# Bank reservation in the score filler, a GELU batch over chunks 3 and 4, and a new transpose estimate, in a two-layer attention and gMLP kernel

## The chip, the cores and the metric

The kernel runs on one core of one Trainium2 chip. The metric is the device time of one execution in microseconds (us), as the median of several runs. A ratio below is the mean time of one kernel's runs over the mean of the other's in the same rounds, so it is not quite the ratio of the medians quoted next to it. For every run the mean granted TensorE clock is recorded too (1.0 is full speed).

## The reference

Two layers, each an attention block and a gated mixer over x of 2048 x 512, bf16:

```python
def _A_ref(x, wq, wk, wv, wo):            # 32 heads of 16, one shared key and value head
    q = (x @ wq).reshape(B, S, 32, 16).transpose(0, 2, 1, 3)
    k = x @ wk;  v = x @ wv
    scores = einsum('bhqd,bkd->bhqk', q, k) * 16 ** -0.5
    o = einsum('bhqk,bkd->bhqd', softmax(scores), v)
    return o.transpose(0, 2, 1, 3).reshape(B, S, 512) @ wo
def _B_ref(x, w_in, w_sp, b_sp, w_out):
    z = gelu(x @ w_in)                    # 512 -> 1792
    z1 = z[..., :896]; z2 = layernorm(z[..., 896:])
    g = einsum('ts,bsf->btf', w_sp, z2) + b_sp[None, :, None]   # mixes tokens
    return (z1 * g) @ w_out
x = x + _A(layernorm(x)); x = x + _B(layernorm(x))      # twice, same weights
```

## The kernel before

The Python program holds a list scheduler. It models five engines in time (PE is TensorE, ACT ScalarE, DVE VectorE, POOL GpSimd, SP the DMA queue), and whenever a modelled engine is free it commits the ready operation of the lowest priority number. What it emits is a fixed order for each engine, with semaphore waits. So every number in the model can change the whole order.

A layer takes the queries in six chunks (512, 512, 512, 256, 128, 128 tokens). For each chunk come the scores, the exponentials, the products with V, the output projection, and then the first part of the mixer: two products with w_in, GELU, and the layernorm of z2. The product with w_sp runs in passes over the tiles of 128 tokens as they come ready: tiles 0 to 7 after chunk 1, 8 to 11 after chunk 2, 12 to 14 after chunk 4 (the "early pass"), tile 15 in the closing stage.

The exponentials, 4096 score blocks of 128 keys by 512 columns (tokens, or tokens times heads), are shared. Most go to ScalarE (an exp activate over 3 or 2 blocks). The others go to VectorE, which has a chain of seven instructions for them. A VectorE block rides along with a score fill: it takes one of the two side PSUM banks that all other products also use.

```python
class DexStream:
    def take(self, t, js):           # called when a score fill is committed: a VectorE block too?
        if sc.bank_free() > t:
            return None
        base = 2 * (self.nb % (NPD // 2))
        if not self.batch:
            ...
            backlog = sc.free["dve"] - t + sum(o.dur for o in sc.ready["dve"] ...)
            if backlog > BACKLOG:            # 3 us
                return None
        ...
    def limit(self, layer):          # no VectorE blocks in a layer's last units
        return len(self.k.units) * (layer + 1) // 2 - ENDX
```

GELU needs another ScalarE table set than exp, so it is done in batches. The products are copied out first; then one batch activates them in place. Chunks 0 and 1 share a batch; chunks 2, 3 and 4 have one each; chunk 5 activates straight from PSUM.

```python
def mixer_chunk(self, g):
    ...
    if g.ci == 0:
        self.held = (T, z1, z2, z1v)
        return
    zs = [(T[0], n, z1v)]
    if g.ci == 1:
        T, z1, z2 = [a + b for a, b in zip(self.held[:3], (T, z1, z2))]
        zs = [(T[0], n, self.held[3])] + zs
    ...
    def gl(e):
        for (_t, _n, v) in zs:
            e.activation(v, v, ACTF.Gelu_apprx_tanh)
        return e.activation(z2f[:, t0 * FH:(t0 + nt) * FH], z2f[...], ACTF.Gelu_apprx_tanh)
```

A DMA transpose is modelled as 1.25 us of issue, plus its bytes, plus 1.9 us until it is visible:

```python
def transpose(self, out, src, deps, sem, pr):
    return self.dma(lambda e: e.dma_start_transpose(out, src), deps, sem, 131072, pr, issue=1.25)
```

The softmax here doesn't subtract the row's maximum and nothing guards it: scores larger than these inputs give would overflow.

## Time and profile before

| | before |
|---|---|
| median time | 1871.99 us (3 runs, 1869.53 to 1872.58) |
| span of the profiled run | 1867.6 us |
| last exp of layer 0, of layer 1 | 880.5 us, 1812.6 us |
| score blocks on ScalarE, on VectorE | 3595, 501 |
| table loads | 21 |

These are lines of the page of before. The first gives busy us, share of the span and number of instructions of each engine. The others are groups of instructions: line, engine, operation, tiles and shapes, count, then busy us and mean ns of one, then the idle time just before them and what ended most of it.

```profile
PE 1595.0 (85%) x11889; PEld 477.3 (26%) x11889; DVE 1736.9 (93%) x3107; ACT 1756.6 (94%) x1581; POOL 53.4 (3%) x94
...
L1343 ACT ACTIVATE Pa<-ps_all 128x1536 bf16<-128x1536 f32 (+1 forms) x1439 | 1637.5, 1368 | 31.1 <-PE ps_all L1615 16.2
...
L1520 DVE TENSOR_SCALAR E<-ps_all 128x512 int32<-128x512 f32 x501 | 341.1, 683 | 28.8 <-PE ps_all L1615 26.3
```

Two engines are full. The 3595 blocks of ScalarE take 1637.5 us, 0.455 us each; the count of the last line is the number of blocks that VectorE takes.

The groups of ScalarE, kept apart by shape, show the table loads of the GELU batches (to GELU, and back to exp):

```profile
L993 ACT ACT_TABLE_LOAD x8 | 10.3, 1283 | 0.1
L1343 ACT ACT_TABLE_LOAD x8 | 10.3, 1283 | 0.1
```

The timeline of ScalarE around the batches of chunks 3 and 4 in layer 0. Its columns are start, time until the group's end, engine, line, operation; in brackets is the idle time before it and its releaser.

```profile
808.03 1.28 ACT L993 ACT_TABLE_LOAD   x1
809.32 1.70 ACT L993 ACTIVATE z1s<-z1s 128x1792 bf16<-128x1792 bf16 x1
810.93 1.68 ACT L994 ACTIVATE z2n<-z2n 128x1792 bf16<-128x1792 bf16 x1
812.62 1.28 ACT L1343 ACT_TABLE_LOAD   x1
813.92 19.29 ACT L1343 ACTIVATE Pa<-ps_all 128x1024 bf16<-128x1024 f32 x17
833.52 16.35 ACT L1343 ACTIVATE Pa<-ps_all 128x1536 bf16<-128x1536 f32 x14 [0.31 <-PE ps_all L1615]
...
852.44 1.28 ACT L993 ACT_TABLE_LOAD   x1
853.73 0.95 ACT L993 ACTIVATE z1s<-z1s 128x896 bf16<-128x896 bf16 x1
854.59 0.93 ACT L994 ACTIVATE z2n<-z2n 128x896 bf16<-128x896 bf16 x1
855.54 1.28 ACT L1343 ACT_TABLE_LOAD   x1
```

ScalarE runs through both batches without a pause.

Two stretches by engine (from:to in us, length, then busy us and instructions of each engine, granted TensorE clock, share and GB/s of DMA). The first lies in the steady part, the second holds chunk 4's batch.

```profile
core 0: us, PE busy (x) PEld busy (x) DVE busy (x) ACT busy (x) POOL busy (x), PEclk, DMA share, GB/s
93.00:117.00 24.00, 18.97 (x151) 4.76 (x144) 23.79 (x42) 23.94 (x22) 0.00 (x0) 1.00 0.00 1
846.00:857.00 11.00, 9.26 (x88) 3.79 (x86) 9.02 (x17) 10.76 (x11) 0.00 (x0) 1.00 0.05 12
```

### The profile page before, as it was taken

To read this page: it belongs to the slowest core of one execution; us is meant where nothing else is said; L and a number is where in the kernel's file an instruction comes from. 1 tells how busy PE (TensorE), PEld (TensorE's weight loads), DVE (VectorE), ACT (ScalarE), POOL (GpSimd) and SP (SyncE) were. 2 spreads that over 40 slices of the span, in tenths; PEclk is the share of its full clock that TensorE was granted. 3 is DMA by queue.
4 is the path that set the end of the run, shared out by engine and by line. 5 is a ranking of instruction groups with operands and counts; after the bars stand their busy time and mean duration, and the time that the engine had idled before them with its cause. 6 is when DMAs were issued, how large, how long until landed. Compare 5 with 4: busy or idle time off the path is not lost.

```text
span 1867.6 us, 30386 instructions
## 1 busy us (share of the span) xinstructions
PE 1595.0 (85%) x11889; PEld 477.3 (26%) x11889; DVE 1736.9 (93%) x3107; ACT 1756.6 (94%) x1581; POOL 53.4 (3%) x94
## 2 busy tenths in 40 slices
PE   8777888878889988989887778887788799999898
PEld 3222222212222222223432122222222222222234
DVE  8999999999879999997889999999999689989978
ACT  8999999999989999998579999999999899999983
POOL 2000000000000000000100000000000000000000
PEclk9999999999989999999999999999999899999999
DMA  9700010000010020221210000000000100111213
GB/s 272 197 1 1 12 35 1 1 1 18 7 40 24 23 46 1 66 70 48 66 33 1 1 1 12 10 26 1 5 13 7 40 24 24 46 43 35 62 45 110
DMA packets 125142, 68.58 MB, mean 37 GB/s; under 512 B 79172, under 2 KB 121416, under 8 KB 125000
## 3 DMA queue, kind: packets, MB, share of 16 engines
q1 hardware_dynamic: 123416, 66.48, 13.2%
q8 instruction: 95, 1.56, 0.3%
q14 instruction: 47, 0.39, 0.1%
q10 hardware_dynamic: 1584, 0.16, 0.1%
HBM read 30.97 MB, written 17.83 MB: 26 GB/s over the span
## 4 chain that ended last, share of the span: by engine, by line
ACT 36%; DVE 30%; PE 18%; issue 14%; POOL 1%; ACTq 0%; POOLq 0%; DVEq 0%
ACT Pa L1343 34%; PE ps_all L1088 6%; PE ps_all L1615 5%; DVE E L1520 5%; DVE Pd L1558 4%; PE ps_all L1419 3%; DVE E L1556 2%; DVE E L1553 2%; DVE E L1547 2%; DVE gp L1100 2%; PE ps_all L1177 1%; DVE st L622 1%; DVE E L1550 1%; DVE E L1549 1%; DVE z2n L937 1%
## 5 line engine op out<-in xcount | busy, mean ns | idle before, releaser
L1343 ACT ACTIVATE Pa<-ps_all 128x1536 bf16<-128x1536 f32 (+1 forms) x1439 | 1637.5, 1368 | 31.1 <-PE ps_all L1615 16.2
L1615 PE MATMUL ps_all<-qs,kT 32*128 32x512 bf16 x4096 | 566.5, 387 | 226.3 <-ACT Pa L1343 206.6
L1520 DVE TENSOR_SCALAR E<-ps_all 128x512 int32<-128x512 f32 x501 | 341.1, 683 | 28.8 <-PE ps_all L1615 26.3
L1615 PEld LDWEIGHTS ps_all<-qs,kT 32*128 32x128 bf16 x4096 | 139.3, 91 | 779.3 <-ACT Pa L1343 728.7
L1419 PE MATMUL ps_all<-Pa,V 128*32 128x512 bf16 x3595 | 324.9, 388 | 1.5 <-DVE Pd L1558 0.6
L1558 DVE SCALAR_TENSOR_TENSOR Pd<-E 128x1024 uint16<-128x1024 int32 x251 | 304.4, 1213 | 1.1
L1601 PE MATMUL ps_all<-zero 128*128 128x512 bf16 x817 | 263.3, 393 | 2.1 <-POOL zero L585 1.0
L1088 PE MATMUL ps_all<-wsT,z2n 128*128 128x512 bf16 x714 | 199.0, 383 | 6.5 <-DVE E L1520 2.6
L1419 PE MATMUL ps_all<-Pd,V 128*32 128x512 bf16 x501 | 177.7, 389 | 0.0
L1553 DVE TENSOR_TENSOR E<-E 128x1024 f16<-128x1024 f16 x251 | 171.3, 682 | 3.4
L1556 DVE TENSOR_TENSOR E<-E 128x1024 f16<-128x1024 f16 x251 | 171.0, 681 | 2.5
L1547 DVE TENSOR_SCALAR E<-E 128x1024 f16<-128x1024 uint16 x251 | 171.1, 682 | 1.6
L1549 DVE TENSOR_SCALAR E<-E 128x1024 f16<-128x1024 f16 x251 | 104.5, 416 | 2.2
L1550 DVE TENSOR_SCALAR E<-E 128x1024 f16<-128x1024 f16 x251 | 104.3, 415 | 2.3
L1601 PEld LDWEIGHTS ps_all<-zero 128*128 128x128 bf16 x817 | 62.7, 98 | 138.0 <-issue 116.8
L1419 PEld LDWEIGHTS ps_all<-Pa,V 128*32 128x32 bf16 x3595 | 65.3, 94 | 125.4 <-issue 114.3
L1100 DVE TENSOR_TENSOR gp<-ps_all,gp 128x512 f16<-128x512 f32 x112 | 75.0, 682 | 21.8 <-PE ps_all L1088 21.8
L1088 PEld LDWEIGHTS ps_all<-wsT,z2n 128*128 128x128 bf16 x714 | 54.5, 97 | 105.2 <-issue 54.8
L784 PE MATMUL ps_all<-xnTA,wq_pad 128*128 128x512 bf16 (+2 forms) x384 | 72.4, 313 | 2.0 <-DVE qs L793 1.3
L962 PE MATMUL ps_all<-xnTB,w_in_r 128*128 128x512 bf16 (+2 forms) x336 | 62.6, 310 | 5.2 <-DVE z1s L973 2.3
L926 PE MATMUL ps_all<-w_in_r,xnTB 128*128 128x448 bf16 x256 | 63.4, 356 | 3.5 <-DVE z2n L937 1.4
L1177 PE MATMUL ps_all<-E 128*128 128x512 bf16 x224 | 53.6, 380 | 4.2 <-ACT E L1156 3.6
(87 smaller groups left out, 1013.9 us busy)
## 6 DMA issues: line engine op xcount, KB each, us to landing
wsT_scratch<-gp SPq DMA_DIRECT2D x16, 512.0 KB, 3.6
wsT<-wsT_scratch SPq DMA_DIRECT2D x8, 1024.0 KB, 5.4
z1s<-z_scratch SPq DMA_DIRECT2D x16, 448.0 KB, 3.8
wsT<-wsT_scratch SPq DMA_DIRECT2D x8, 512.0 KB, 3.4
z_scratch<-z1s SPq DMA_DIRECT2D x4, 896.0 KB, 5.2
X<-in_A_x_dram SPq DMA_DIRECT2D x8, 256.0 KB, 5.3
out_dram<-X SPq DMA_DIRECT2D x16, 128.0 KB, 1.9
w_in_r<-in_B_w_in_dram SPq DMA_DIRECT2D x1, 1792.0 KB, 10.3
```

The lines of the kernel that those rows point to most:

```text
L1088: ins = e.matmul(self.b32(b), self.z2n[:, s, f * 128:(f + 1) * 128], w_[:, s - s0, :], start=st, stop=sp)
L1343: return e.activation(k.Pa[:, base:base + n, :], k.b32(b0, n).rearrange("p (k q) -> p k q", k=n), ACTF.Exp, scale=SCALE)
L1419: ins = e.matmul(k.b32(k.pvb)[32 * j:32 * j + 32, :], k.V[:, u.kt, 32 * j:32 * j + 32], b.slot, tile_position=(0, 32 * j), start=u.first, ...
L1520: return k.sc.op("dve", lambda e: e.tensor_scalar(k.eI[:, s, 512 * i:512 * (i + 1)], k.b32(j.bank.idx)[:, 0:512], C_LOG2, C_BIAS, op0=ALU. ...
L1547: return lambda e: e.tensor_scalar(out, a, m, None, op0=ALU.mult)
L1549: return lambda e: e.tensor_scalar(out, a, b, None, op0=ALU.add)
L1550: return lambda e: e.tensor_scalar(out, a, m, b, op0=ALU.mult, op1=ALU.add)
L1553: o4 = sc.op("dve", lambda e: e.tensor_tensor(q, u, w, ALU.mult), d_sb(n, 0.521e-3), [o3], pr)
L1556: o6 = sc.op("dve", lambda e: e.tensor_tensor(q, q, u, ALU.mult), d_sb(n, 0.521e-3), [o5], pr)
L1558: o7 = sc.op("dve", lambda e: e.scalar_tensor_tensor(po.bitcast(U16), I, 2.0 ** -9, q, op0=ALU.mult, op1=ALU.add), d_sb(n, 1.042e-3), [o6] ...
L1601: return e.matmul(k.b32(k.pvb if b is None else b.idx), k.zero[:], k.zero[:, None, :].to_broadcast([P, 4, P]), start=b is not None, stop=b ...
L1615: return e.matmul(self.b32(bank), self.kT[32 * j:32 * j + 32, kt * 128:(kt + 1) * 128], self.qs[32 * j:32 * j + 32, g.q.slot, :], tile_pos ...
```

## The change

The intent has three parts. (1) The GELU of chunks 3 and 4 becomes one batch, so a switch of tables there and back goes away in each layer. (2) A score fill takes no side bank for a VectorE block while urgent products wait for one, or while products of the early pass wait, so that the ends of the layers run sooner. (3) The scheduler takes a DMA transpose to land about 1 us sooner. The diff, cut to its core:

```diff
-            o.vis = self.dma_free + 1.9
+            o.vis = self.dma_free + (1.9 if o.lat is None else o.lat)
...
+URGENT = 1.0
...
+        self.gelus = [(0, 1), (2,), (3, 4), (5,)]
...
     def transpose(self, out, src, deps, sem, pr):
-        return self.dma(lambda e: e.dma_start_transpose(out, src), deps, sem, 131072, pr, issue=1.25)
+        return self.sc.op("sp", lambda e: e.dma_start_transpose(out, src), 1.2, deps, pr, sem=sem, dma=131072, lat=0.9)
...
+        batch = [b for b in self.gelus if g.ci in b][0]
...
-            z1v = self.z1s[:].rearrange("p (f t) -> p f t", f=NF)[:, :, 0:n]
+            z1v = self.z1s[:].rearrange("p (f t) -> p f t", f=NF)
+            z1v = z1v[:, :, 256:256 + n] if g.ci == 4 else z1v[:, :, 0:n]
...
-        if g.ci == 0:
-            self.held = (T, z1, z2, z1v)
+        self.held.append((T, z1, z2, (T[0], n, z1v)))
+        if g.ci != batch[-1]:
             return
+        T, z1, z2 = [[x for h in self.held for x in h[i]] for i in range(3)]
+        zs = [h[3] for h in self.held]
...
+                if early:
+                    self.early_first.append(sc.first_op)
...
         base = 2 * (self.nb % (NPD // 2))
+        if any(o.start is None and o.ready is not None and o.ready <= t for o in k.early_first):
+            return None
+        want = sum(o.first and o.prio < URGENT and o.ready <= t for o in sc.ready["pe"])
+        if want and sum(not b.busy and not b.closed and b.free_at <= t for b in sc.banks) <= want:
+            return None
```

The diff also adds a second weight slab for passes of more than 8 tiles. The passes are not changed and none has more than 8, so that code is never reached.

## The prediction

> What bounds it now. The page's busy times: ScalarE 1756.6 us (94% of 1867.6), VectorE 1736.9 (93%), TensorE 1595.0 (85%). Both softmax engines are full together: in 23.4 us stretches away from the layer ends, ScalarE is busy 23.3 and VectorE 22.7 to 23.1. By the groups, ScalarE exponentiates 3595 score blocks in 1637.5 us (0.455 us each), VectorE 501 blocks at about 2.7 us each. So a microsecond saved on ScalarE is worth about 0.86 us of span (2.2 blocks/us of 2.57), and each block VectorE does not take costs ScalarE 0.455 us. About 110 us of ScalarE idling lie in the start and the two layer ends (885-957, 1813-1867.6), which are latency chains over VectorE, PSUM and TensorE.
>
> What the change does.
> (1) GELU of chunks 3 and 4 becomes one batch (0 and 1 already are). Per layer one GELU and one exp table load go: the groups show ACT_TABLE_LOAD at 1283 ns, so 2.57 us per layer, plus some 0.2 us for a merged activate; 5.5 us of ScalarE in all, worth about 4.7 us. The Trainium skill, "ScalarE: Activation LUTs" (What ACT_TABLE_LOAD costs), gives the same 1283 ns, plus a drain of about 1.38 us; the timeline here shows the neighbours back to back with the loads, so I count no drain. Price: chunk 3's layernorm statistics (4 at 0.6 us) move behind chunk 4's, starting the early spatial pass some 3 us later.
> (2) The score filler takes no side bank for a VectorE block while urgent products (priority under 1: chunks 3 to 5's w_in products, first q sets, first keys) are as many as the free banks, or early-pass (tiles 12 to 14) products wait. Chunk 4 now needs from X at 833.6 to GELU at 852.4 (19 us), its z2 evicted only at 845.5; I expect 3 to 6 us less. VectorE loses blocks there, estimated 6 to 14 over both layers: +2 to +5 us. In the early pass itself VectorE takes no block already (0 from 850 to 890).
> (3) The early pass ends now at 892 and 1825, after the last exp (880.5, 1812.6); its last evictions (0.69 us each) interleave with the last chunk's residual, statistics and normalisation. Starting 1 to 3 us earlier net, it gives 1 to 2 us per layer end.
> (4) The list scheduler assumes DMA transposes to land 1 us sooner. Issue to landing measures 2.4 to 2.5 us, nearer the new number (about 2.65) than the old (3.7): dependents move up in TensorE's order; worth 0 to 2 us, no stalls.
> Passes and chunk sizes are unchanged; passes have at most 8 tiles, so the added second weight slab is never used. Rescheduling I take as noise of 5 us either way.
>
> Sum: -4.7 +3.5 -3 -1, about -6 us (estimate).
>
> Predicted 1865 us, range 1852 to 1880; faster by over 2%: 0.03; within 2%: 0.95; slower by over 2%: 0.02.
>
> What would show each step. Table loads 21 -> 17 in the groups. VectorE blocks 501 -> about 490, ScalarE's up by as many, its busy time about 1755 us. Chunk 4's residual to GELU shorter by 3 to 6 us; last early eviction nearer the last exp. Layer-end idle of ScalarE 1 to 2 us shorter each. No TensorE waits for transposes.
>
> What would make it wrong. The bank rule blocks VectorE much longer (40 blocks lost: +16 us); the merged batch delays the early pass so that the closing waits; the closing tails, 35 to 40 us of idle each, reschedule well (15 us faster) or badly.

## More of the kernel before

TensorE is kept warm: where the modelled work of the last 3.41 us falls under a threshold plus `WARM = 800` columns, a matmul of zeros is put in.

One line of the waits: who waited for whom, us in total, times, longest.

```profile
PE ps_all L895 <- DMA onT<-on: 0.4, 1, 0.4
```

## The result, and the profile after

| | before | after |
|---|---|---|
| median time (4 runs each) | 1872.28 us (1869.53 to 1874.53) | 1862.49 us (1859.6 to 1863.22) |
| span of the profiled run | 1867.6 us | 1860.5 us |
| to the last exp of layer 0 / from there to that of layer 1 / tail | 880.5 / 932.1 / 55.0 us | 878.7 / 927.7 / 54.1 us |
| blocks on ScalarE, VectorE | 3595, 501 | 3601, 495 |
| table loads | 21 | 17 |
| mean granted clock of the profiled run | 0.990 | 0.982 |

The ratio is 0.9945, with a 95% interval of 0.9928 to 0.9963: half a per cent faster, well clear of noise and well inside 2%.

The lines of the page of after:

```profile
PE 1580.7 (85%) x11768; PEld 475.0 (26%) x11851; DVE 1724.1 (93%) x3086; ACT 1751.7 (94%) x1574; POOL 49.4 (3%) x90
...
L1362 ACT ACTIVATE Pa<-ps_all 128x1536 bf16<-128x1536 f32 (+1 forms) x1441 | 1638.8, 1363 | 28.9 <-PE ps_all L1639 26.5
...
L1544 DVE TENSOR_SCALAR E<-ps_all 128x512 int32<-128x512 f32 x495 | 336.5, 683 | 27.5 <-PE ps_all L1639 25.3
```

ScalarE's groups by shape: two loads each way are gone.

```profile
L997 ACT ACT_TABLE_LOAD x6 | 7.7, 1283 | 0.1
L1362 ACT ACT_TABLE_LOAD x6 | 7.7, 1283 | 0.1
```

The timeline of ScalarE around the grouped batch of layer 0, up to the last exp of the layer:

```profile
843.57 1.28 ACT L997 ACT_TABLE_LOAD   x1
844.87 2.54 ACT L997 ACTIVATE z1s<-z1s 128x1792 bf16<-128x1792 bf16 x2
847.31 2.43 ACT L998 ACTIVATE z2n<-z2n 128x2688 bf16<-128x2688 bf16 x1
849.75 1.28 ACT L1362 ACT_TABLE_LOAD   x1
851.05 3.71 ACT L1362 ACTIVATE Pa<-ps_all 128x1536 bf16<-128x1536 f32 x3
856.77 21.94 ACT L1362 ACTIVATE Pa<-ps_all 128x1024 bf16<-128x1024 f32 x20 [2.01 <-PE ps_all L1639]
878.73 1.28 ACT L1378 ACT_TABLE_LOAD   x1
```

The same two stretches of after:

```profile
core 0: us, PE busy (x) PEld busy (x) DVE busy (x) ACT busy (x) POOL busy (x), PEclk, DMA share, GB/s
93.00:117.00 24.00, 19.36 (x148) 4.61 (x140) 23.09 (x40) 22.97 (x22) 0.00 (x0) 0.93 0.00 1
846.00:857.00 11.00, 4.45 (x20) 1.19 (x24) 10.83 (x23) 8.96 (x8) 1.58 (x2) 0.53 0.42 108
```

Here is something that the prediction did not have. TensorE's order is the same in both kernels over the first 1484 matmuls (to 229 us), and yet the stretch from 93 to 117 us was granted a clock of 0.93 instead of 1.00, and ScalarE did 22.97 us of work in it instead of 23.94. That alone is no difference between the kernels: the profile of before has such a stretch of half clock too, at 148.1 us, and run 12, which has the order of after, has three up to there (98.2, 149.4 and 200.6 us, two of them twice as long). Where the half-clock stretches fall differs between executions of one order. And behind the grouped batch, where ScalarE works for 7.5 us without any exp and TensorE has little to do (4.45 us busy of 11), the clock fell to 0.53; the exps then waited 2.01 us for scores. That was seen in this place in a kernel without the grouping too (the bank rule alone, 0.80 from 860 to 884 us), so the grouping is not its only cause.

The Trainium skill, "TensorE: Matmul & The Clock Gate" (Part 1), says that the gate looks at activity in a free-running window of 3413 ns and halves the clock after an idle one. The traces agree with the window: in each profile all stretches at half clock start on one grid of 3.413 us, and all last 3.41 us or a multiple of it, but for two that the end of the kernel cuts off. They do not agree that the window before must be idle: before nine of the twelve such stretches of after, TensorE was busy for 0.40 to 0.70 of the window, and its longest pause was 2.29 us.

The waits of TensorE for transposed tiles grew:

```profile
PE ps_all L899 <- DMA onT<-on: 3.8, 3, 2.3
```

### The profile page after: what moved, and what is told of

Its sections match the earlier page's. It is cut to its first block, busy times and chain, and to the rows that moved or that the text cites. A ratio compares the mean times of both kernels' runs of the same rounds, so it can differ in the third digit from the quotient of the medians. Undisturbed runs are those within 1.5% of the kernel's fastest.

```text
span 1860.5 us, 30195 instructions
## 1 busy us (share of the span) xinstructions
PE 1580.7 (85%) x11768; PEld 475.0 (26%) x11851; DVE 1724.1 (93%) x3086; ACT 1751.7 (94%) x1574; POOL 49.4 (3%) x90
## 4 chain that ended last, share of the span: by engine, by line
ACT 41%; PE 21%; DVE 21%; issue 16%; DMA 1%; POOL 0%; ACTq 0%; POOLq 0%
ACT Pa L1362 39%; PE ps_all L1104 6%; PE ps_all L1639 6%; PE ps_all L1438 4%; DVE E L1544 3%; DVE Pd L1582 2%; DVE E L1571 2%; DVE E L1577 2%; PE ps_all L1196 2%; DVE E L1580 1%; PE ps_all L1625 1%; DVE st L626 1%; ACT z2n L998 1%; DVE E L1573 1%; DVE E L1574 1%
## 5 line engine op out<-in xcount | busy, mean ns | idle before, releaser
L1544 DVE TENSOR_SCALAR E<-ps_all 128x512 int32<-128x512 f32 x495 | 336.5, 683 | 27.5 <-PE ps_all L1639 25.3
L1582 DVE SCALAR_TENSOR_TENSOR Pd<-E 128x1024 uint16<-128x1024 int32 x248 | 300.6, 1212 | 1.0
L1625 PE MATMUL ps_all<-zero 128*128 128x512 bf16 x779 | 253.3, 399 | 2.4 <-DVE E L1544 1.0
L1104 PE MATMUL ps_all<-wsT,z2n 128*128 128x512 bf16 x658 | 188.6, 382 | 9.4 <-issue 4.8
L1577 DVE TENSOR_TENSOR E<-E 128x1024 f16<-128x1024 f16 x248 | 169.0, 681 | 3.0
L1580 DVE TENSOR_TENSOR E<-E 128x1024 f16<-128x1024 f16 x248 | 169.2, 682 | 2.4
```

What stands on the lines that cost most here:

```text
L1104: ins = e.matmul(self.b32(b), self.z2n[:, s, f * 128:(f + 1) * 128], w_[:, s - s0, :] if s - s0 < na or not spare else wsp[:, s - s0 - na, :],
L1544: return k.sc.op("dve", lambda e: e.tensor_scalar(k.eI[:, s, 512 * i:512 * (i + 1)], k.b32(j.bank.idx)[:, 0:512], C_LOG2, C_BIAS, op0=ALU. ...
L1577: o4 = sc.op("dve", lambda e: e.tensor_tensor(q, u, w, ALU.mult), d_sb(n, 0.521e-3), [o3], pr)
L1580: o6 = sc.op("dve", lambda e: e.tensor_tensor(q, q, u, ALU.mult), d_sb(n, 0.521e-3), [o5], pr)
L1582: o7 = sc.op("dve", lambda e: e.scalar_tensor_tensor(po.bitcast(U16), I, 2.0 ** -9, q, op0=ALU.mult, op1=ALU.add), d_sb(n, 1.042e-3), [o6] ...
L1625: return e.matmul(k.b32(k.pvb if b is None else b.idx), k.zero[:], k.zero[:, None, :].to_broadcast([P, 4, P]), start=b is not None, stop=b ...
```

## The experiments

What could make up the 10 us? Theory A is the sum of the prediction: every part has its own worth, most of it the table loads. Rival B says that a list scheduler that is nudged gives another order, and that the gain is luck of the order. Rival C says that the loads are hidden. Two more came up on the way: D, that the granted clock explains the differences between runs; and E, that the GELU grouping and the bank rule need each other, against F, that the parts simply add.

All twelve runs ran to the end. Eleven gave correct results; one is wrong. The times were taken in five rounds each, so 5 or 6 executions, against 11 of before on the same chip. "Mean clock" is the mean over a kernel's runs; before's is 0.9878 over 33 runs. The kernel after was timed with 4 runs of before. It was run at another time. Each kernel was profiled in one of its executions; places and stretches below are read from that one, which for runs 3, 4, 9 and 12 is the slowest of the run and for run 11 the fastest.

| run | median us | ratio to before (95%) | mean clock |
|---|---|---|---|
| after (from the result) | 1862.49 | 0.9945 (0.9928 to 0.9963) | 0.9825 |
| 1 GELU grouping alone | 1872.46 | 1.0008 (0.9994 to 1.0023) | 0.9818 |
| 2 bank rule alone | 1871.35 | 1.0003 (0.9989 to 1.0018) | 0.9832 |
| 3 transpose estimate alone | 1864.89 | 0.9967 (0.9955 to 0.9979) | 0.9866 |
| 4 before, four loads away, same order | 1870.12 | 0.9996 (0.9984 to 1.0008) | 0.9884 |
| 5 before, nudged by 1 ns (a) | 1873.86 | 1.0016 (1.0003 to 1.0029) | 0.9857 |
| 6 before, nudged by 1 ns (b) | 1870.22 | 0.9989 (0.9975 to 1.0002) | 0.9808 |
| 7 before, more warming | 1874.10 | 1.0020 (1.0005 to 1.0035) | 0.9885 |
| 8 after, more warming | 1867.59 | 0.9974 (0.9959 to 0.9988) | 0.9897 |
| 9 grouping and rule | 1869.79 | 0.9992 (0.9979 to 1.0005) | 0.9838 |
| 10 grouping and estimate | 1869.65 | 1.0001 (0.9988 to 1.0015) | 0.9780 |
| 11 rule and estimate | 1868.17 | 0.9988 (0.9970 to 1.0007) | 0.9840 |
| 12 after, four loads back, same order | 1869.04 | 0.9991 (0.9975 to 1.0007) | 0.9805 |

### 1. The GELU grouping alone

After, with its two new tests in `take` taken out and the old transpose:

```diff
-        if any(o.start is None and o.ready is not None and o.ready <= t for o in k.early_first):
-            return None
-        want = ...
-        if want and ... <= want:
-            return None
...
-        return self.sc.op("sp", lambda e: e.dma_start_transpose(out, src), 1.2, deps, pr, sem=sem, dma=131072, lat=0.9)
+        return self.dma(lambda e: e.dma_start_transpose(out, src), deps, sem, 131072, pr, issue=1.25)
```

> The kernel before with the GELU grouping alone (no bank rule, old transpose estimate). Theory A, the parts add up as predicted: 17 table loads, VectorE blocks 501 give or take 4, and 4 to 5 us less than before (ratio 0.9973 to 0.9979). Rival B, the gain of the whole change is luck of the rescheduled order: anything from -8 to +8 us, with the difference not at chunks 3 and 4 but spread over stretches whose work is the same. Rival C, table loads are hidden: 0.

It had 17 loads and 503 VectorE blocks, and it was not faster: 1.0008. Theory A's 4 to 5 us did not show in the time. Its mean clock was 0.9818 against 0.9878. Counted in finished score blocks, it was 4.8 us ahead of before at block 1920, but only 0.2 us ahead at block 2048, the last exp of layer 0. All kernels with the grouping and the usual warming show this pair in layer 0: 5.3 to 7.1 us shorter from block 1664 to 1920, 3.8 to 6.9 us longer from there to 2048. Most of it is no gain: chunk 3's batch has moved from the first stretch into the second.

### 2. The bank rule alone

Before, with the two tests in `take` and the list of the early pass's first operations:

```diff
+                if early:
+                    self.early_first.append(sc.first_op)
...
         base = 2 * (self.nb % (NPD // 2))
+        if any(o.start is None and o.ready is not None and o.ready <= t for o in k.early_first):
+            return None
+        want = sum(o.first and o.prio < URGENT and o.ready <= t for o in sc.ready["pe"])
+        if want and sum(not b.busy and not b.closed and b.free_at <= t for b in sc.banks) <= want:
+            return None
```

> The kernel before with the bank rule alone. Theory A: VectorE blocks about 490, chunk 4's residual to GELU 3 to 6 us shorter, early pass nearer the last exp, span -3 to +2 us. Rival B: as large a change as from any perturbation, -8 to +8 us, not tied to chunks 3 to 5. If the rule carries the gain of the whole change: -8 to -10 us.

VectorE took 497 blocks, 4 fewer. The time from chunk 4's residual to its GELU load (read from the timelines, 18.8 and 19.0 us in the two layers of before) was 19.4 and 17.3 us; 3 to 6 us less had been expected. The time did not change: 1.0003. The rule alone is worth nothing here.

### 3. The transpose estimate alone

```diff
-            o.vis = self.dma_free + 1.9
+            o.vis = self.dma_free + (1.9 if o.lat is None else o.lat)
...
-        return self.dma(lambda e: e.dma_start_transpose(out, src), deps, sem, 131072, pr, issue=1.25)
+        return self.sc.op("sp", lambda e: e.dma_start_transpose(out, src), 1.2, deps, pr, sem=sem, dma=131072, lat=0.9)
```

> The kernel before with the new transpose estimate of the scheduler alone. Theory A: 0 to -2 us, no TensorE waits for transposes, the change in the layer turn. Rival B: -8 to +8 us with changes all over.

This is the only part that gained by itself: 0.9967, about 6 us. It did not come without stalls. TensorE now reaches the output projection before its transposed tiles, as in after:

```profile
PE ps_all L895 <- DMA onT<-on: 2.6, 2, 1.8
```

The profiled execution is the slowest of its five (1869.15 us at a clock of 0.982; the others took 1862.8 to 1865.2 at 0.987 to 0.988), no faster than the profiled one of before (1869.40), so the trace can't show where the 6 us lie. What moved is the order of the mixer's work. The GELU batch of chunks 0 and 1 began, with its table load, at 495.0 us, with 1208 blocks done, instead of 503.3 us with 1236. Every kernel with the new estimate and the usual warming starts it at block 1208 in layer 0 (runs 3, 10, 11, 12 and after); every one with the old estimate, no nudge and the usual warming starts it at 1236. The stretch from block 1024 to 1408 was 2.5 us shorter here (5.1 in after, 5.8 and 4.6 in runs 10 and 11; 0.6, 0.8 and 1.6 longer in runs 1, 2 and 9). But the stretch behind it, to block 1664, gave back 2.8 to 4.6 us in all four, so this shift does not by itself explain the 6 us. And run 12 tells how little such a stretch is worth: it has the order of after, and its stretch was 1.6 us longer than before's, 6.7 us longer than after's. These are the two stretches by engine (columns as above; after, then run 12). The clock was 0.97 and 0.92:

```profile
419.90:591.60 171.70, 145.80 (x1057) 42.53 (x1065) 159.48 (x283) 168.71 (x141) 4.67 (x6) 0.97 0.08 24
422.10:600.40 178.30, 152.76 (x1056) 43.02 (x1065) 159.78 (x283) 169.46 (x140) 4.75 (x6) 0.92 0.08 23
```

### 4. The loads taken away from before, order kept

```diff
+            fn3 = ACTF.Exp if g.ci == 3 else ACTF.Gelu_apprx_tanh
             for (_t, _n, v) in zs:
-                e.activation(v, v, ACTF.Gelu_apprx_tanh)
-            return e.activation(z2f[:, t0 * FH:(t0 + nt) * FH], z2f[...], ACTF.Gelu_apprx_tanh)
+                e.activation(v, v, fn3)
+            return e.activation(z2f[:, t0 * FH:(t0 + nt) * FH], z2f[...], fn3)
```

> The kernel before, same order on every engine, with exp in place of gelu in chunk 3's batch alone, so no table switch there (17 loads instead of 21); the result is wrong on purpose. It measures the four loads by themselves. Theory A: each 1.28 us load is on the path, -5 us (ratio 0.9973). Rival C, loads are hidden by the fixed order of VectorE and TensorE: 0 to -1 us.

The result is wrong (exp in place of gelu in chunk 3's batch). 17 loads, the same order on every engine, and no gain: 0.9996. Rival C holds in this place. ScalarE's timeline shows where the 2.57 us went:

```profile
808.58 1.69 ACT L994 ACTIVATE z1s<-z1s 128x1792 bf16<-128x1792 bf16 x1
810.17 1.69 ACT L995 ACTIVATE z2n<-z2n 128x1792 bf16<-128x1792 bf16 x1
811.75 2.36 ACT L1344 ACTIVATE Pa<-ps_all 128x1024 bf16<-128x1024 f32 x2
815.33 1.02 ACT L1344 ACTIVATE Pa<-ps_all 128x1024 bf16<-128x1024 f32 x1 [1.22 <-PE ps_all L1616]
817.68 16.21 ACT L1344 ACTIVATE Pa<-ps_all 128x1536 bf16<-128x1536 f32 x14 [1.33 <-PE ps_all L1616]
```

The loads are gone, and in their place ScalarE waits 1.22 and 1.33 us, 2.55 together, for scores that TensorE could not produce earlier, because it waits for VectorE to empty the side banks. One of TensorE's own waits in between, before the second of them:

```profile
816.70 0.60 PE L1089 MATMUL ps_all<-wsT,z2n 128*128 128x512 bf16 x2 [0.87 <-DVE gp L1101]
```

In before these waits were hidden behind the loads. ScalarE was busy without a pause there, and still it was not what the next microsecond depended on.

Since the order is the same, each activate of this run can be laid beside its twin in before. In layer 0 the run was 0.67 us late when the batch came, 2.16 us early at the first exp behind it, and 0.68 us late again six exps later; in layer 1 it was 2.62 us late, then 0.23 early, then 2.63 late. No half-clock stretch lies in these places in either profile. So in place the loads are worth 0.0 us, far below the noise of the whole time. The 3.5 us by which the profiled run was longer in all came elsewhere, 1.8 us of it about 1455 us, where it had 8 windows at half clock and before 4.

### 5 and 6. Two nudges without meaning

```diff
 def d_psum(n):
-    return n * 1.042e-3 + 0.066
+    return n * 1.042e-3 + 0.067
```

```diff
-LAT = {"pe": 0.22, ...
+LAT = {"pe": 0.221, ...
```

> Control: the kernel before with the scheduler's estimate of a PSUM read on VectorE longer by 1 ns (0.067 us instead of 0.066), which has no meaning for the chip but reorders the program. Theory A (parts have their own worth, reordering is small): within 3 us of before. Rival B (reordering is luck as large as the change): off by 5 to 10 us either way. Theory D (runs differ through the granted clock, about 1 us per 0.001 of mean clock within one kernel): the time follows the mean clock of the run.

> Second control: the kernel before with the scheduler's latency of TensorE results longer by 1 ns. The same expectations: A within 3 us, B off by 5 to 10 us, D time follows the mean clock.

The first was 2.2 us slower by the medians, the second 1.4 us faster (3.0 and 2.1 us by the ratios), so in raw time these two new orders cost or gave 2 to 3 us. The first is just beyond noise (1.0003 to 1.0029). Runs 1, 2, 9, 10 and 11 lie in the same band, run 11 at its edge. Of the parts, their pairs and the whole, only run 3 and the whole change lie outside it.

Theory D was met within each kernel, not between kernels: the second nudge was the faster one with a clock lower by 0.0070 than before's. Taking each of the 105 runs against the mean of its own kernel, time and mean clock go together with a correlation of -0.94: 0.001 less clock is 1.09 us more. A clock 0.001 lower means about 3.7 us more at half clock (2 x 0.001 x 1867), so a microsecond at half clock costs about 0.29 us. Before is on the favourable side: its mean clock is 0.9878, and of the other orders in the table only those with more warming, and run 4, which is before's own order, reach it. By this slope the whole change gives back about 5.8 us (0.0053 of clock); that is an estimate, since the slope is from runs within a kernel and is here used between kernels. By the same slope the second nudge, which means nothing, would be 9.6 us faster than before at equal clock, against about 15 us for the whole change (both are estimates). So at equal clock, luck of the order alone came to nearly two thirds of the gain.

### 7 and 8. More warming

```diff
-WARM = 800.0
+WARM = 1400.0
```

> The kernel before with more warming matmuls (margin 1400 columns instead of 800; 1114 such matmuls instead of about 817). Theory D: half-clock time falls from about 1.2% of the span, mean clock from 0.988 to 0.993 or more, and the time by about 3 to 5 us. Rival: the extra matmuls get in the way of the score fills, 0 to +5 us although the clock rises.

> The changed kernel with the same larger margin (1073 warming matmuls instead of about 779). Theory D: the changed kernel gives back about 6 us through its lower clock (0.9825 against 0.988), so here the mean clock rises to 0.99 or more and the time falls to 1852 to 1857, more than the same margin gives to the kernel before. Rival: no gain, 1860 to 1867.

(The 1.2% in the expectation is the share of the clock that was lost; the time at half clock is twice that.) Theory D does not lead to a better kernel this way. In before the clock hardly rose (0.9885) and the time rose by 2.4 us. In after the clock did rise, to 0.9897, but the median was 1867.59: the new order and the extra matmuls together cost more than the clock gave; which of the two, no run separates. Its best run, 1860.5 us at a clock of 0.994, is no better than after at 0.982. VectorE took only 487 blocks in it.

### 9, 10 and 11. The pairs

Run 9 is after with the old transpose lines:

```diff
-        return self.sc.op("sp", lambda e: e.dma_start_transpose(out, src), 1.2, deps, pr, sem=sem, dma=131072, lat=0.9)
+        return self.dma(lambda e: e.dma_start_transpose(out, src), deps, sem, 131072, pr, issue=1.25)
```

Run 10 is after without the two tests in `take`:

```diff
-        if any(o.start is None and o.ready is not None and o.ready <= t for o in k.early_first):
-            return None
-        want = sum(o.first and o.prio < URGENT and o.ready <= t for o in sc.ready["pe"])
-        if want and sum(not b.busy and not b.closed and b.free_at <= t for b in sc.banks) <= want:
-            return None
```

Run 11 is before with the edits of runs 2 and 3 together, as they stand above.

> The changed kernel with the old transpose estimate: GELU grouping and bank rule together. The grouping alone gained 5 us by block 1920 and lost it at the layer turn, where its early pass ended 17.5 us after the last exp (11.8 in before). Theory E (the bank rule keeps the early pass in time, so the two need each other): last early eviction within 13 us of layer 0's last exp, the layer turn (last exp of layer 0 to block 2112) at most 1 us longer than before's 89.6, and 3 to 6 us less than before in all at equal clock. Theory F (the parts simply add: 0.9 and -0.2 us): +1 give or take 2 us.

> The changed kernel without the bank rule: GELU grouping and transpose estimate. Theory E: the early pass is late again (15 us or more after layer 0's last exp), the layer turn 5 us or more longer than before's 89.6, the time 3 to 6 us above the whole change (1865 to 1868). Theory F: 0.9 - 6.7, about 1866 as well, but without a late early pass.

> The changed kernel without the GELU grouping (21 table loads): bank rule and transpose estimate. Theory E: the grouping is worth its 5 us when the rule is there, so 4 to 6 us above the whole change (1866 to 1868). Theory F: -0.2 - 6.7, 1864 to 1866. Rival B, the whole gain is luck of the order: anything from 1860 to 1876.

Theory E falls. In run 9, with the rule, the early pass still ended 17.6 us after layer 0's last exp, and yet the layer turn, from the last exp to block 2112, was just 0.1 us longer than before's 89.6 us. In run 10, without the rule, the early pass ended 14.3 us after it in layer 0 and the turn was 0.2 us longer; the grouping alone had 17.5 us and a turn 7.7 us longer. So a late early pass does not by itself make a long turn, nor is a long turn tied to the parts: the first nudge had one of 102.7 us, with the pass ending 18.7 us after the last exp. Two of E's numbers came close and are not explained by it: run 9 is about 5 us faster than before at equal clock by the slope (3 to 6 expected), and run 11 took 1868.17 us (1866 to 1868). Run 10 took 1869.65, outside both ranges. E also rested on a misreading: run 1 had lost its gain by layer 0's last exp, before the turn. In run 10 something else was lost: its tail behind layer 1's last exp took 62.8 us instead of 55.0, with the early pass ending 26.1 us after the last exp. But run 1 had 24.9 us there, and a tail of 55.0.

Theory F falls too. The three parts alone sum to -0.2% and the whole is -0.55%, while each pair is within 0.12% of before. Averaged over its four pairs of kernels with and without it, in mean times, the grouping is worth 0.0 us (+1.7, -1.1, +5.9, -6.6), the rule -2.0 us and the estimate -4.8 us (-0.6, -2.2 and -4.8 us by the ratios, which take out what differs between the chips). Corrected to before's clock with the slope above, these are -4 us, -2 us and -6 us; with controls that lie 10 us apart once corrected in that way (+0.8 and -9.6 us), that says little.

### 12. The loads put back into after, order kept

```diff
-            for (_t, _n, v) in zs:
+            for i_, (_t, _n, v) in enumerate(zs):
+                if i_ == 1 and g.ci == 4:
+                    e.activation(self.tiny[:], self.mhalf[:], ACTF.Exp)
                 e.activation(v, v, ACTF.Gelu_apprx_tanh)
```

> The changed kernel, same order on every engine, with one tiny exp between the two z1 activates of the grouped batch, so that the exp and the GELU table load come back there, 2.77 us more in each layer. If ScalarE is the bound in that place (no VectorE blocks are taken any more after the batch): +4 to +5.5 us. If VectorE and TensorE hold it in their fixed order, as in the run without loads: 0 to +1.5 us.

Here ScalarE's timeline in layer 0, to be laid beside that of after:

```profile
850.45 1.28 ACT L999 ACT_TABLE_LOAD   x1
851.74 1.70 ACT L999 ACTIVATE z1s<-z1s 128x1792 bf16<-128x1792 bf16 x1
853.44 1.28 ACT L998 ACT_TABLE_LOAD   x1
854.74 0.20 ACT L998 ACTIVATE tiny<-mhalf 128x1 f32<-128x1 f32 x1
854.94 1.28 ACT L999 ACT_TABLE_LOAD   x1
856.24 0.95 ACT L999 ACTIVATE z1s<-z1s 128x896 bf16<-128x896 bf16 x1
...
866.48 21.94 ACT L1364 ACTIVATE Pa<-ps_all 128x1024 bf16<-128x1024 f32 x20 [1.94 <-PE ps_all L1641]
888.44 1.28 ACT L1380 ACT_TABLE_LOAD   x1
```

From the first load to the end of the layer's exps after needs 35.16 us (843.57 to 878.73); here it is 37.99 (850.45 to 888.44), 2.83 us more. In layer 1 the same stretch is 33.64 and 36.68, 3.04 us more. The wait for scores is 2.01 and 1.94 us: it did not shrink. So in this place the two loads and the tiny activate cost all of their 2.77 us, 5.9 us in both layers. VectorE starts just one block behind this batch in layer 0 (at 853.2 us, here 863.0) and none in layer 1, so nearly all exps to the end of the layer are left to ScalarE. Activate by activate the result is the same: this run was 6.87 us behind after before the batch and 9.78 behind at the first exp after it, 9.79 and 12.71 in layer 1, so 2.9 us each time.

The time rose from a ratio of 0.9945 to 0.9991, about 8.6 us (6.5 us by the medians), where 4 to 5.5 were expected if ScalarE is the bound. 5.9 us of it is these loads; the mean clock was 0.0020 lower, which is 2.2 us by the slope.

## Why the prediction was right or wrong

The time was right: 1865 predicted, 1862.49 measured, inside 1852 to 1880, and "within 2%" held. The direction and size, about -6 us, met -9.8 by the medians. But the sum was right for partly other reasons: of its four terms, none was shown at its size, and that they came together near the measured time is in good part luck.

- **Loads, 21 to 17: right. Their worth of about 4.7 us: not shown, and the reason given was wrong.** The prediction took each microsecond of ScalarE as worth 0.86 us because ScalarE was busy throughout. Taken away in before's order at chunk 3's batch, the loads were worth 0.0 us in place (ratio 0.9996); the same two loads added at the layer's end cost 2.83 and 3.04 us. The worth of a load depends on where it stands, and the one that was removed stood where VectorE and TensorE held the pace. That its removal becomes worth something once the whole is reordered is possible, but over four pairs of kernels the grouping averages 0.0 us (-0.6 by the ratios).
- **VectorE's blocks, 501 to about 490: right.** It was 495, and ScalarE's count rose by 6, at the low end of the 6 to 14 estimated. ScalarE's busy time was 1751.7 us, 1755 predicted.
- **Chunk 4 sooner by 3 to 6 us: mis-sized.** From its residual to its GELU load it took 16.0 and 18.4 us instead of 18.8 and 19.0, so 2.8 and 0.6 us less.
- **The early pass nearer the last exp, layer ends shorter by 1 to 2 us each: not met.** It ended 11.1 and 12.6 us after the last exp, 11.8 and 12.8 before. ScalarE's idle time in the 85 us after layer 0's last exp rose from 36.5 to 39.2 us; the tail fell by 0.9 us. The runs with a late early pass show no fixed price for it.
- **The transpose estimate, 0 to 2 us, no TensorE waits: wrong on both.** It was the largest part alone (0.9967) and the largest on average (-4.8 us), and it made TensorE wait 3.8 us for the transposed attention tiles (0.4 in before). The issue-to-landing time itself is the same before and after: 2.5 us for the attention tiles, 2.4 us for the mixer's. What it changed is the order.
- **What was left out: the clock.** The prediction had no term for the half-clock windows. Between before and after the mean clock fell from 0.9878 to 0.9825, by the slope within kernels some 5.8 us. Rescheduling "noise of 5 us either way" was about the right size, but part of it comes in through the clock.

What stays open: why all three parts together give 10 us when no pair gives more than 3. No control had so large a gain in raw time, but there were only two, one of them 9.6 us faster at equal clock by the estimate above, and after is one of eight combinations, so luck of the order is not ruled out. Why before's order draws fewer half-clock windows than the others is not settled either. And no run here beats after.

## What to carry to other kernels

An engine without pauses is not thereby the bound: take the suspected work away in a fixed order and see whether a wait appears in its place, before counting its time as a gain. Where a program is ordered by a scheduler, run several meaningless nudges of it first, since their spread (here 5 us of 1870 between two of them, 10 us at equal clock) is what a part's gain must exceed, and record the granted clock with each time. Where two runs have the same order, lay them beside each other instruction by instruction: the shift before and after a place gives its worth to a tenth of a microsecond, when the whole times differ by several. Parts measured alone need not add up, so measure the pairs as well before crediting a part.

## What the Trainium skill lacked or had wrong

- "ScalarE: Activation LUTs" (What ACT_TABLE_LOAD costs): the load of 1283 ns agrees with every trace here. The 1.38 us of drain on top of it does not show: two loads and a tiny activate put into a fixed order cost 2.83 and 3.04 us, where two switches of 2.66 us would be over 5.
- The same page, and its advice to group by table set: it does not say that a switch can be free. At chunk 3's batch the four loads of the two layers were worth 0.0 us, in the grouped batch two more in each layer cost all of their time, 2.9 us.
- "TensorE: Matmul & The Clock Gate" (Part 1 and Terms): the window of 3413 ns agrees. Part 1 names an idle window as what brings the half clock; here TensorE was busy for 0.40 to 0.70 of the window before nine of after's twelve half-clock stretches. Under Terms it gives the penalty as half of the throttled time; in this kernel, which TensorE does not bound, it was less: 0.29 us for each us at half clock, from 1.09 us for 0.001 of mean clock over 105 runs.
- No page says what warming matmuls cost a kernel that TensorE does not bound: with 1400 instead of 800 columns after's mean clock rose from 0.9825 to 0.9897 and its median from 1862.49 to 1867.59 us. The order changed with it, so the cost of the matmuls alone is not shown.
